# Decode attention beside a gated MLP: the last head's third and fourth V tiles in one load, with dummy matmuls in the wait

## The chip, the core and the metric

The kernel runs on one NeuronCore of a Trainium2 chip. Its engines are the tensor engine (PE; its weight loads are listed as PEld), the vector engine (DVE), the scalar engine (ACT), GpSimd (POOL) and the sync engine (SP), which here issues the large transfers. Sixteen DMA engines bring data from device memory into the on-chip buffer. The metric is the device time of one execution in microseconds (us), taken as the median of several executions. The profile of one execution counts from its first to its last instruction, which is a little less than the device time.

## The reference, cut to what matters

One decode step: a single token `x` of width 1024, attention with 32 query heads over 4 key/value heads of 65,536 positions, and a small gated MLP, mixed by a sigmoid gate.

```python
q = (x @ wq)                                   # 32 heads of 128
k = jnp.repeat(k_cache, 8, axis=1)             # k_cache, v_cache: 4 heads x 65536 x 128, bf16
v = jnp.repeat(v_cache, 8, axis=1)
scores = einsum('bhqd,bhkd->bhqk', q, k) * 128 ** -0.5
p = softmax(scores)
o = einsum('bhqk,bhkd->bhqd', p, v)
a = o.reshape(1, 1, 4096) @ wo                 # wo: 4096 x 1024
# b: the gated MLP of the same token (w_in 1024 x 3584, w_out 1792 x 1024)
out = g * a + (1 - g) * b                      # g = sigmoid(sum(x * gate_w))
```

The two caches are 67 MB each, and the three large weights and `wo` add some 28 MB, all read once.

## The kernel before

The caches are read in tiles of 4 MB (128 partitions x 32 KB), four to a head for K and four for V. All of them, and the weights, go through one buffer `kv` of five such slots. A load names the slot at which it begins and is issued by SP once the earlier users of the slots are done.

```python
kv = big.tile([P, NKV * CT * P], BF16, name="kv")      # NKV = 5 slots, P = CT = 128

def load_kv(src, g, j, at, n=1):                       # n tiles in one transfer, from slot `at`
    ...
    v = load(rows[:, i * CT * DH:(i + n) * CT * DH], (n * CT * DH,), at)
    return [v[:, i * CT * DH:(i + 1) * CT * DH] for i in range(n)]

def v_tile(g, j, vt):                                  # L464: 32 matmuls, 16 weight loads
    for u in range(CC // 2):
        hs = slice(u % 2 * P // 2, (u % 2 + 1) * P // 2)   # two halves of the PE's columns
        for e in range(2):
            nc.tensor.matmul(o_ps[g][hs, e, :], lhsT=ptt[g, j][:, 2 * u:2 * u + 2, :]...,
                             rhs=vx[:, 2 * u + e], ...)    # 128x64 weights, 512 columns

def keep_busy(n):                                      # L503: n matmuls whose result nobody reads
    ps = pss.tile([P, 2 * HN], FP32, name="busy_ps", tag="s")
    ...
    for i in range(n):
        nc.tensor.matmul(ps[:, :HN], lhsT=w[:, :P], rhs=w[:, :HN], start=True, stop=True, ...)
```

`keep_busy` computes nothing: it only keeps PE working, so that its clock isn't lowered. `head_out` ends a head: a masked product of the accumulated output (L474) and a sum (L478) on DVE, two small matmuls (L482 and L484) on PE, and five short DVE operations that end in `oa`, the head's part of the vector that meets `wo`. The tail of the program is:

```python
for j, n, at in ((0, 2, 2), (2, 1, 1), (3, 1, 0)):     # last head's V: tiles 0+1, 2, 3
    for i, vt in enumerate(load_kv(A_v_cache, G - 1, j, at, n)):
        v_tile(G - 1, j + i, vt)
keep_busy(6)
head_out(G - 1)
keep_busy(16)

c0 = 0
for n in WO_SPLIT:                                     # (24, 4, 2, 1, 1) of 32 rows of wo per partition
    t = load(wo_view[:, c0:c0 + n, :], (n, D), 3 + c0 * D / (CT * P))     # from slot 3 on
    project(t, n, oa, c0, last=(c0 + n == OC))         # L514: 4 matmuls of 256 columns per row
    keep_busy(WO_BUSY[n])                              # {24: 0, 4: 2, 2: 1, 1: 0}
    c0 += n
nc.scalar.copy(out=out_sb[:], in_=out_ps[:])           # L566
# two small stores of out_sb
```

[...]SP issues all loads on one queue. The four tiles of the last head's V are called V0 to V3 below.

Of the kernel before, what the change touches and what calls it, by code (L numbers as in the profile page):

```python
# [29 lines left out]
def kernel(  # L30
# [18 lines left out]
    _, G, S, DH = A_k_cache.shape  # L49
# [30 lines left out]
    def same_weights(ins):  # L80
        held.add(ins.ins.name)
# [95 lines left out]
    def load(src, shape, at):  # L177
        n = 1
        for s in shape:
            n *= s  # L180
        v = kv[:, int(at * CT * P):int(at * CT * P) + n]
        if len(shape) == 2:
            v = v.rearrange("p (a b) -> p a b", b=shape[1])
        ins = nc.sync.dma_start(out=v, in_=src)  # L184
        if not first_load:
            first_load.append(ins.ins.name)
        return v

    def load_kv(src, g, j, at, n=1):
        h, i = divmod(j, 2)  # L190
        rows = src[0, g, 2 * h * CT * P:2 * (h + 1) * CT * P, :].rearrange(
            "(p c) d -> p (c d)", c=2 * CT)
        v = load(rows[:, i * CT * DH:(i + n) * CT * DH], (n * CT * DH,), at)
        return [v[:, i * CT * DH:(i + 1) * CT * DH] for i in range(n)]
# [166 lines left out]
    for k in range(NHB):  # L361
# [3 lines left out]
                                                                   j=B, e=2),  # L365
# [91 lines left out]
    def v_tile(g, j, vt):  # L457
        if j == 0:
            o_ps[g] = pso.tile([P, 2, VC * DH], FP32, name="o_ps")
        vx = vt.rearrange("p (v c d) -> p c v d", v=VC, d=DH)  # L460
        for u in range(CC // 2):
            hs = slice(u % 2 * P // 2, (u % 2 + 1) * P // 2)
            for e in range(2):
                ins = nc.tensor.matmul(  # L464
                    o_ps[g][hs, e, :],
                    lhsT=ptt[g, j][:, 2 * u:2 * u + 2, :].rearrange("p c x -> p (c x)"),
                    rhs=vx[:, 2 * u + e], start=(j == 0 and u < 2),
                    stop=(j == NT - 1 and u >= CC // 2 - 2), skip_group_check=True)
                if e > 0:
                    same_weights(ins)  # L470

    def head_out(g):
        gs = slice(g * B, (g + 1) * B)
        nc.vector.tensor_tensor(  # L474
            out=om8, in0=o_ps[g][:].rearrange("p e (v d) -> p (e v) d", d=DH),
            in1=own_8[:].unsqueeze(2).to_broadcast([P, 2 * VC, DH]), op=ALU.mult)
        o_sb = wk.tile([P, DH], FP32, name="o_sb")
        nc.vector.tensor_reduce(out=o_sb[:], in_=om8.rearrange("p x d -> p d x"), axis=AX.X,  # L478
                                op=ALU.add)
        om_ps = psm.tile([P, DH + NT], FP32, name="om_ps", tag="m")  # L480
        hs = hsel[:].rearrange("p h q -> p (h q)")
        nc.tensor.matmul(om_ps[gs, DH:], lhsT=hs, rhs=lss[g][:], start=True, stop=True,  # L482
                         skip_group_check=True)
        nc.tensor.matmul(om_ps[gs, :DH], lhsT=hs, rhs=o_sb[:], start=True, stop=True,  # L484
                         skip_group_check=True)
        rl = wk.tile([P, 2], FP32, name="rl")
        nc.vector.reduce_sum(out=rl[gs, 0:1], in_=om_ps[gs, DH:], axis=AX.X)
        nc.vector.reciprocal(out=rl[gs, 1:2], in_=rl[gs, 0:1])
        om = wk.tile([P, QD, OC], FP32, name="om")
        nc.vector.tensor_tensor(  # L490
            out=om[gs], in0=om_ps[gs, :DH].rearrange("p (q c) -> p q c", c=OC),
            in1=own_q[gs, :].unsqueeze(2).to_broadcast([B, QD, OC]), op=ALU.mult)
        osum = wk.tile([P, OC], FP32, name="osum")
        nc.vector.tensor_reduce(out=osum[gs, :], in_=om[gs].rearrange("p q c -> p c q"),
                                axis=AX.X, op=ALU.add)
        nc.vector.tensor_scalar(out=oa[gs, :], in0=osum[gs, :], scalar1=rl[gs, 1:2],
                                scalar2=gate[gs, :], op0=ALU.mult, op1=ALU.mult)

    def keep_busy(n):
        ps = pss.tile([P, 2 * HN], FP32, name="busy_ps", tag="s")  # L500
        w = wt[G % 2][:].rearrange("p v b t u h -> p (v b t u h)")
        for i in range(n):
            ins = nc.tensor.matmul(ps[:, :HN], lhsT=w[:, :P], rhs=w[:, :HN], start=True,  # L503
                                   stop=True, skip_group_check=True)
            if i > 0:
                same_weights(ins)
# [22 lines left out]
    for g in range(1, G):  # L529
# [16 lines left out]
            if h == 0 and g + 1 < G:  # L546
                build_w(g + 1)
        head_out(g - 1)
    for j, n, at in ((0, 2, 2), (2, 1, 1), (3, 1, 0)):
        for i, vt in enumerate(load_kv(A_v_cache, G - 1, j, at, n)):  # L550
            v_tile(G - 1, j + i, vt)
    keep_busy(6)
    head_out(G - 1)
    keep_busy(16)


    wo_view = A_wo.rearrange("(p c) n -> p c n", c=OC)
# [52 lines left out]
```

## Time and profile before

The time before is 381.88 us, the median of 3 executions (381.71 to 381.96); the profiled span is 380.5 us.

| what | busy us | share of the span |
|---|---|---|
| PE matmuls | 226.4 | 60% |
| PE weight loads | 55.6 | 15% |
| DVE | 211.2 | 56% |
| ACT | 39.6 | 10% |
| POOL | 4.4 | 1% |
| DMA queue of SP | 16 engines | 98.8% |

The DMA engines moved 162.17 MB at a mean of 426 GB/s. Busy time on an engine says little where it works beside another; the reader should first look at which resource has no gaps, and then at the chain of waits that ended last. Granted clock means the share of PE's full clock that the chip allowed it at that moment; in this profile it stands at 1.00 or at 0.50.

### The profile page before, as it was taken

To read this page: it belongs to the slowest core of one execution; us is meant where nothing else is said; L and a number is where in the kernel's file an instruction comes from. 1 tells how busy PE (TensorE), PEld (TensorE's weight loads), DVE (VectorE), ACT (ScalarE), POOL (GpSimd) and SP (SyncE) were. 2 spreads that over 40 slices of the span, in tenths; PEclk is the share of its full clock that TensorE was granted. 3 is DMA by queue.
4 is the path that set the end of the run, shared out by engine and by line. 5 is a ranking of instruction groups with operands and counts; after the bars stand their busy time and mean duration, and the time that the engine had idled before them with its cause. 6 is when DMAs were issued, how large, how long until landed. Compare 5 with 4: busy or idle time off the path is not lost.

```text
span 380.5 us, 2602 instructions
## 1 busy us (share of the span) xinstructions
PE 226.4 (60%) x1397; PEld 55.6 (15%) x800; DVE 211.2 (56%) x207; ACT 39.6 (10%) x55; POOL 4.4 (1%) x10
## 2 busy tenths in 40 slices
PE   0060605967655784794499139762993197739386
PEld 0010101211211210121022001110220011202113
DVE  4134217989374947867893058678940397650040
ACT  1001000111104310114011001140110010500000
POOL 4000000000000000000000000000000000000000
PEclk9995765999958796999599758995898599959789
DMA  9999999999999999999999999999999999999995
GB/s 386 476 420 413 401 442 441 441 472 410 407 422 441 441 443 434 434 434 441 441 429 441 434 441 420 422 413 442 434 434 429 427 434 442 436 410 434 431 432 224
DMA packets 3655, 162.17 MB, mean 426 GB/s; under 512 B 440, under 2 KB 444, under 8 KB 828
## 3 DMA queue, kind: packets, MB, share of 16 engines
q1 hardware_dynamic: 3604, 162.01, 98.8%
q8 instruction: 8, 0.13, 0.1%
q14 instruction: 3, 0.02, 0.0%
q10 hardware_dynamic: 40, 0.01, 0.0%
HBM read 162.01 MB, written 0.00 MB: 426 GB/s over the span
## 4 chain that ended last, share of the span: by engine, by line
DMA 71%; PE 17%; DVE 9%; issue 2%; SPq 0%; ACTq 0%; ACT 0%; DVEq 0%
DMA kv<-in_A_k_cache_dram 52%; PE s_ps L419 13%; DVE kv L412 8%; DMA kv<-in_A_wo_dram 7%; DMA kv<-in_A_v_cache_dram 7%; DMA wb<-in_B_b_sp_dram 5%; PE o_ps L464 2%; PE z_ps L296 1%; SPq L184 0%; DVE mx L402 0%; ACTq L198 0%; PE small_ps L271 0%; ACT out_sb L566 0%; PE out_ps L514 0%; ACTq L199 0%
## 5 line engine op out<-in xcount | busy, mean ns | idle before, releaser
L419 PE MATMUL s_ps<-kv,wt 128*128 128x512 bf16 x512 | 132.8, 414 | 81.4 <-DVE kv L412 81.3
L412 DVE STREAM_TRANSPOSE kv<-kv 128x2048 int32<-128x2048 int32 x64 | 142.4, 2280 | 69.7 <-DMA kv<-in_A_k_cache_dram 69.7
L464 PE MATMUL o_ps<-kv,pt 128*64 128x512 bf16 x512 | 63.6, 408 | 14.3 <-DMA kv<-in_A_v_cache_dram 14.3
L419 PEld LDWEIGHTS <-wt 128*128 128x128 bf16 x256 | 26.4, 103 | 189.2 <-issue 117.9
L428 ACT CAST sc<-s_ps 128x1024 bf16<-128x1024 f32 x16 | 16.2, 1013 | 250.7 <-PE s_ps L419 250.7
L464 PEld LDWEIGHTS <-pt 128*64 128x64 bf16 x256 | 16.9, 117 | 57.9 <-issue 48.6
L454 DVE STREAM_TRANSPOSE pt<-sc 128x1024 bf16<-128x1024 bf16 x16 | 18.6, 1217 | 6.8 <-ACT sc L451 6.8
L474 DVE TENSOR_TENSOR rowt<-o_ps,own 128x1024 f32<-128x1024 f32 x4 | 4.8, 1195 | 26.5 <-PE o_ps L464 26.5
L451 ACT ACTIVATE sc<-sc,nb 128x1024 bf16<-128x1024 bf16 x16 | 18.2, 1137 | 12.2 <-DVE nb L447 12.2
L484 PE MATMUL om_ps<-o_sb,hsel 128*32 128x128 f32 x8 | 2.3, 388 | 18.3 <-DVE o_sb L478 18.3
L402 DVE TENSOR_TENSOR mx<-mx,sc 128x1024 bf16<-128x1024 bf16 x8 | 5.5, 687 | 13.6 <-ACT sc L428 13.6
L296 PE MATMUL q_ps<-kv,xT 128*32 128x512 bf16 x64 | 5.7, 534 | 7.2 <-DMA kv<-in_A_wq_dram 7.2
L252 PE MATMUL xb_ps<-xg,spread 8*128 8x256 bf16 x1 | 0.4, 364 | 13.5 <-DMA xg<-in_gate_w_dram 13.5
L478 DVE TENSOR_REDUCE o_sb<-rowt 128x128 f32<-128x1024 f32 x4 | 7.5, 1872 | 0.1
L363 DVE TENSOR_TENSOR rowt<-q_ps,own_b 128x512 f32<-128x512 f32 x2 | 1.3, 686 | 10.8 <-PE q_ps L296 10.8
L503 PE MATMUL busy_ps<-wt 128*128 128x512 bf16 x25 | 6.1, 381 | 0.0
L296 PE MATMUL z_ps<-kv,xT 128*32 128x448 bf16 x64 | 6.1, 572 | 0.0
L566 ACT CAST out_sb<-out_ps 128x256 bf16<-128x256 f32 x1 | 0.4, 372 | 46.4 <-PE out_ps L514 46.4
L256 DVE TENSOR_TENSOR xm<-xb_ps,sel_i 128x128 f32<-128x128 f32 x2 | 0.5, 286 | 8.2 <-PE xb_ps L252 8.2
L514 PE MATMUL out_ps<-kv,oa 128*32 128x256 bf16 x128 | 4.2, 273 | 1.4 <-DMA kv<-in_A_wo_dram 1.4
L435 DVE TENSOR_REDUCE m<-mx 128x1 f32<-128x1024 bf16 x4 | 4.8, 1209 | 0.1
L296 PEld LDWEIGHTS <-xT 128*32 128x32 bf16 x64 | 2.6, 137 | 14.7 <-issue 14.6
(90 smaller groups left out, 61.2 us busy)
## 6 DMA issues: line engine op xcount, KB each, us to landing
kv<-in_A_v_cache_dram SPq DMA_DIRECT2D x2, 4096.0 KB, 22.8
kv<-in_B_w_in_dram SPq DMA_DIRECT2D x1, 7168.0 KB, 19.7
kv<-in_A_wo_dram SPq DMA_DIRECT2D x1, 6144.0 KB
kv<-in_B_w_out_dram SPq DMA_DIRECT2D x1, 3584.0 KB
kv<-in_A_wo_dram SPq DMA_DIRECT2D x1, 1024.0 KB, 26.8
kv<-in_A_wo_dram SPq DMA_DIRECT2D x1, 512.0 KB
kv<-in_A_wo_dram SPq DMA_DIRECT2D x2, 256.0 KB
kv<-in_A_k_cache_dram SPq DMA_DIRECT2D x8, 27.6
```

Of the source, the lines that this page charges most:

```text
L296: ins = nc.tensor.matmul(ps[t * B:(t + 1) * B, k * HN:k * HN + n], lhsT=xT[:, i * KH + c:i * KH + c + 1].to_broadcast([P, B]), rhs=w[:, c, ...
L402: nc.vector.tensor_tensor(out=mx[:], in0=mxs[g][:], in1=sc[:], op=ALU.max)
L412: nc.vector.transpose(out=kb[:, v * n:(v + 1) * n], in_=kb[:, v * n:(v + 1) * n])
L419: ins = nc.tensor.matmul(s_ps[:, k * HN:(k + 1) * HN], lhsT=wt[g % 2][:, v, b].rearrange("p a v h -> p (a v h)"), rhs=kx[:, b // 2, b % 2, ...
L428: nc.scalar.copy(out=sct[g, j][:], in_=s_ps[:])
L435: nc.vector.reduce_max(out=m1[:], in_=mxs[g][:], axis=AX.X)
L451: nc.scalar.activation(out=sct[g, j][:], in_=sct[g, j][:], func=ACT.Exp, scale=SCALE, bias=nb[:, 0:1], accum_out=lss[g][:, j:j + 1])
L454: nc.vector.transpose(out=ptt[g, j][:].rearrange("p c x -> p (c x)"), in_=sct[g, j][:])
L464: ins = nc.tensor.matmul(o_ps[g][hs, e, :], lhsT=ptt[g, j][:, 2 * u:2 * u + 2, :].rearrange("p c x -> p (c x)"), rhs=vx[:, 2 * u + e], sta ...
L474: nc.vector.tensor_tensor(out=om8, in0=o_ps[g][:].rearrange("p e (v d) -> p (e v) d", d=DH), in1=own_8[:].unsqueeze(2).to_broadcast([P, 2 ...
L478: nc.vector.tensor_reduce(out=o_sb[:], in_=om8.rearrange("p x d -> p d x"), axis=AX.X, op=ALU.add)
L503: ins = nc.tensor.matmul(ps[:, :HN], lhsT=w[:, :P], rhs=w[:, :HN], start=True, stop=True, skip_group_check=True)
```

## The change

Before, V2 and V3 come in two loads of 4 MB, into slot 1 and slot 0. After, they come in one load of 8 MB into slots 0 and 1, as the other V tiles do. PE then has nothing real to do between V1 and the landing of that load, and the change fills the wait with 40 dummy matmuls. The dummies behind V3 stay at 6, and those behind `head_out` go from 16 to 4. The results don't change.

```diff
-    for j, n, at in ((0, 2, 2), (2, 1, 1), (3, 1, 0)):
-        for i, vt in enumerate(load_kv(A_v_cache, G - 1, j, at, n)):
+    for j, at in ((0, 2), (2, 0)):
+        for i, vt in enumerate(load_kv(A_v_cache, G - 1, j, at, 2)):
             v_tile(G - 1, j + i, vt)
-    keep_busy(6)
+        keep_busy((40, 6)[j // 2])
     head_out(G - 1)
-    keep_busy(16)
+    keep_busy(4)
```

The purpose is one transfer fewer, and a PE whose clock is still high when the last two tiles arrive.

## The prediction

> **What bounds the kernel now.** I read the page's 40 slices first, for a resource without gaps; then the chain of waits that ended last, cut to its last stage; then PE's timeline of that stage, for the slack beside the chain; and last the granted clock in chosen stretches, because the change is about dummy matmuls.
>
> The slices and the shares of the chain:
>
> ```profile
> PEclk9995765999958796999599758995898599959789
> DMA  9999999999999999999999999999999999999995
> ...
> DMA 71%; PE 17%; DVE 9%; issue 2%; SPq 0%; ACTq 0%; ACT 0%; DVEq 0%
> ```
>
> The DMA row is at 9 in every slice but the last, while the granted PE clock goes up and down: the transfers run without a pause and PE has room. The last 30 us of the chain (start us, length us, what):
>
> ```profile
> 347.98 0.67 PE o_ps L464 x6
> ...
> 350.46 27.89 DMA kv<-in_A_wo_dram
> 378.35 0.04 issue
> 378.39 0.32 PE out_ps L514 x4
> 378.71 0.02 issue
> 378.73 0.37 ACT out_sb L566
> ```
>
> The end of V1's matmuls at 348.65 frees the slots for wo, and the last wo piece lands at 378.35. Those 27.89 us are a queue, not a start: V2 and V3 were issued at 331.01 and still hold the DMA engines. So the end is set by bytes. Behind the last landing only 4 matmuls, a copy and the stores remain. PE's timeline (start us, length us, then in brackets the idle time before it and what ended it):
>
> ```profile
> 339.43 9.20 PE L464 MATMUL o_ps<-kv,pt 128*64 128x512 bf16 x64 [2.11 <-DMA kv<-in_A_v_cache_dram]
> 349.14 3.65 PE L464 MATMUL o_ps<-kv,pt 128*64 128x512 bf16 x32 [0.52 <-DMA kv<-in_A_v_cache_dram]
> 358.86 6.26 PE L464 MATMUL o_ps<-kv,pt 128*64 128x512 bf16 x32 [6.08 <-DMA kv<-in_A_v_cache_dram]
> ...
> 368.68 3.63 PE L503 MATMUL busy_ps<-wt 128*128 128x512 bf16 x16
> 373.41 3.24 PE L514 MATMUL out_ps<-kv,oa 128*32 128x256 bf16 x112 [1.10 <-DMA kv<-in_A_wo_dram]
> ```
>
> V2 takes 3.65 us and V3, after 6.08 us of idleness, 6.26 us: the lower clock. Yet V3's slowness costs nothing now, because DVE's timeline has `oa` ready at 370.09 (L496, 369.79 + 0.30), and the projection has to wait until 373.41 for wo: 3.3 us of slack.
>
> **The clock.** Sampling the granted clock in steps of 0.25 us shows it falling at 333.5, rising at 343.7, falling at 357.4 and rising at 364.2. The intervals, 10.2, 13.7 and 6.8 us, are 3, 4 and 2 times 3.41 us, and all 22 transitions of the run lie on that grid. The stretches below lie on it (stretch, its length, PE busy time, instructions, granted clock, DMA share, GB/s):
>
> ```profile
> 118.44:121.85 3.41, 1.15 (x7) 1.00 1.20 519
> 121.85:125.27 3.42, 0.00 (x0) 0.50 0.84 364
> 159.41:162.82 3.41, 1.51 (x7) 1.00 1.07 461
> 162.82:166.23 3.41, 2.81 (x13) 1.00 0.98 423
> 330.06:333.47 3.41, 1.07 (x12) 1.00 0.87 370
> 333.47:336.88 3.41, 0.20 (x1) 0.50 1.02 442
> 360.77:364.19 3.42, 3.42 (x19) 0.50 1.03 446
> 364.19:367.60 3.41, 2.49 (x17) 1.00 1.07 461
> 371.01:374.43 3.42, 2.32 (x47) 1.00 0.82 338
> ```
>
> The first stretch was 34% busy and the next one is at half clock; the one at 330.06, 31% busy, likewise. The one at 159.41 was 44% busy and the clock stayed. A full stretch (360.77) brings it back. So this trace puts the limit for a fall between 34% and about 42%, the lowest share in a stretch that stayed up after the start-up.
>
> **What the Trainium skill says.** "TensorE: Matmul & The Clock Gate", Part 1, has a free-running window of 3.4 us at whose end the clock is halved or restored: the grid agrees. It names a whole idle window as what lowers the clock; here 31 to 34% busy did it too, and the measurement decides. The same page ("Wait — 56ns, not 53.3ns?") gives 216 ns per matmul of 512 columns at full clock: the 16 dummies here took 3.63 us, 0.227 each with the last one's tail. "DMA: Bandwidth & Descriptors", "Why a DMA increments its semaphore by 16 and not by 1", says that only the full count means that all data has landed. So V2's matmuls can't begin at half a load. The same page's Bandwidth section fits about 2 us fixed cost for each DMA, on another issue path; here it isn't seen between queued loads: V1, V2 and V3 landed by 339.43, 349.14 and 358.86, 9.71 and 9.72 us apart for 4.19 MB each, which is 431 GB/s.
>
> **The change part by part.**
>
> 1. *The load.* The same 8.39 MB go to the same slots. SP waits for the same event (the previous head's tile leaving slot 1), so issue stays at 331.0, with V0 and V1 still in flight for 8 us. One issue of about 0.4 us goes away on SP, which isn't waited for. As to transfer rate: V2 and V3 took 358.86 - 339.43 = 19.43 us. Two 8 MB loads, from one K landing at 261.97 to the next at 300.67, took 38.70 us, 19.35 each. So fusing saves at most an estimated **0.1 us**.
>
> 2. *V2's matmuls* move from 349.14 to the common landing, about 358.8. 3.65 us that were done early are now done late.
>
> 3. *40 dummies* run from 348.7. Spacing at full clock is (3.63 - 0.38)/15 = 0.217 us (0.38: one matmul's length from the page), so 39 x 0.217 + 0.38 = 8.8 us, to 357.5. That leaves about 1.3 us idle, too little for the clock to fall (at least 60% of any 3.41 us is busy). They end before the landing and delay nothing.
>
> 4. *V2 and V3 at full clock*: 32 matmuls start over 3.45 us (a pair per 0.43 us, with the two column halves overlapping), so 64 take 6.9 + 0.2 = 7.1 us, to 365.9. Before, V3 ended at 365.1. So the restored clock pays back nearly all that fusing costs: net **+0.8 us** here. `head_out` follows unchanged, and `oa` comes at 370.9 instead of 370.1, still 2.5 us ahead of wo. On the end: nothing.
>
> 5. *4 dummies instead of 16* run from 369.5 to 370.5, not to 372.3. Until wo lands at 373.4, PE is idle for 2.9 us, where before it was 1.1 us. Here I see the only way from this change to the end. In a window that closes at time e, PE's busy share falls below 34% for e from about 372.85 to 374.6 (for instance 0.6/3.41 = 18% at e = 373.4). That is 1.75 of 3.41 us, about half of all phases of the free-running grid; for the other half the share is near 40%, at the edge of what I measured. If the clock falls, the projection begins at half rate. At full clock its work, read from the start times of the timeline without the waits, runs 3.17 us for the 112 matmuls, 0.59 for two dummies, 0.33 for 8 matmuls, 0.32 for one dummy, 0.12 and 0.30 for the last two fours: 4.83 us, so PE could be done at 378.24, while it ends at 378.71 (378.39 + 0.32) because of the last landing. That is 0.47 us of slack. Half clock from the landing to the end of one grid stretch lasts 2.9 to 3.4 us and loses half of that, 1.4 to 1.7 us. The end moves by **1.0 to 1.2 us**, and by up to 2.5 if a first stretch of work isn't full enough to restore the clock.
>
> Sum: -0.1 from the load, and a chance of about 0.6 times 1.1 = +0.65 from the clock, on 381.9: **382.4 us**. The 0.6 is my choice: half of the phases for certain, and a small part of the half that stands near 40%.
>
> **Rivals.**
> - *One transfer fewer saves its fixed cost* (2 us): 380. The 9.71 us steps at full rate, and DMA at 9 in every slice, speak against it.
> - *V2 and V3 now collide with the end of the chain*: if the clock falls in the wait nevertheless, 64 matmuls take up to 3.4 us cold and then the rest, some 8.6 us, `oa` comes at 372.5, still before wo. It would take a fully cold 13.8 us to reach 377.7 and an end near 386. The dummies speak against it.
> - *Everything is hidden*: the clock stays up on the 40% windows and with luck of phase, 381.8 us.
> - *Half-clock projection*: 382.8 to 384, as in step 5.
>
> **Range and chances.** The floor is the 0.1 us of the load with some scatter (the runs before span 0.25 us), 381.6; the top is a half-clock projection in the median run, 383.1, with 0.3 us for a slower recovery of the clock, 383.4. Two per cent is 7.6 us, and no term comes near it: same 0.985, faster 0.005, slower 0.01.
>
> **What would show it.** Right: the fused load lands at 358.8 +- 0.2; the 40 dummies end near 357.5; the 64 matmuls take about 7.1 us; L496 ends near 370.9; the last wo piece lands within 0.2 us of 378.3; any added time lies after 373, with clock 0.5 in a stretch there and the x112 group longer than 3.24 us. Wrong: a gap in the DMA row after 348; wo issued more than 5 us later; a landing that moves by over a microsecond; or `oa` later than wo, which would make `head_out` the bound.

## The result, and the profile after

| | median | executions | range |
|---|---|---|---|
| before | 381.87 us | 6 | 381.68 to 381.96 |
| after | 383.32 us | 6 | 382.87 to 384.11 |

The ratio is 1.0042, with a 95% interval from 1.0029 to 1.0055: 1.6 us longer, between 1.1 and 2.1. Within 2% the two count as the same; the difference is nevertheless clear, for no execution of after is as short as any of before. Nor do they agree with each other as those of before do: they spread over 1.24 us against 0.28.

The slices of PE's clock and of the DMA engines, and the shares of the chain that ended last, from the page of after:

```profile
PEclk9995655989969796999599759985898598959996
DMA  9999999999999999999999999999999999999983
...
DMA 62%; PE 19%; DVE 14%; issue 3%; ACT 1%; ACTq 0%; DVEq 0%
```

The DMA row now thins out in its last two slices (8 and 3), where before only the last one was below 9. There is time at the end in which no bytes are awaited. The last stage of the chain of waits (start us, length us, what):

```profile
349.30 23.93 DMA kv<-in_A_wo_dram
373.24 0.04 issue
373.28 6.10 PE out_ps L514 x112
379.38 0.32 PE busy_ps L503
379.70 0.15 issue
379.85 0.40 PE out_ps L514 x8
380.25 0.32 PE busy_ps L503
380.57 0.36 PE out_ps L514 x8
```

The chain leaves the DMA at 373.24, the landing of the first wo piece, instead of at 378.35, the landing of the last one. From there PE's own work is the chain to the end. The first wo piece is not late: PE began the projection at 373.41 before. PE's timeline of after, and below it the line of DVE's that ends in `oa` (start us, length us; in brackets the idle time before and what ended it; x39 stands for the 40 dummies, as a few matmul records are missing from a trace):

```profile
349.20 8.81 PE L503 MATMUL busy_ps<-wt 128*128 128x512 bf16 x39
358.74 7.10 PE L464 MATMUL o_ps<-kv,pt 128*64 128x512 bf16 x64 [0.73 <-DMA kv<-in_A_v_cache_dram]
...
369.40 1.04 PE L503 MATMUL busy_ps<-wt 128*128 128x512 bf16 x4
373.28 6.10 PE L514 MATMUL out_ps<-kv,oa 128*32 128x256 bf16 x112 [2.85 <-DMA kv<-in_A_wo_dram]
...
370.50 0.30 DVE L496 TENSOR_SCALAR oa<-osum,rl,gw 32x32 bf16<-32x32 f32 x1
```

V2 and V3 run at full clock as intended, 7.10 us for 64 matmuls. But 112 matmuls of the projection, which took 3.24 us, take 6.10. The clock shows why. Stretches on the grid of 3.41 us, which in this execution lies elsewhere (stretch, length, PE busy time, instructions, granted clock, DMA share, GB/s):

```profile
365.54:368.96 3.42, 1.80 (x11) 1.00 0.92 393
368.96:372.37 3.41, 1.38 (x6) 1.00 0.77 324
372.37:375.78 3.41, 2.50 (x48) 0.50 0.97 390
375.78:379.19 3.41, 3.41 (x72) 0.50 0.27 102
```

The stretch that ends at 372.37 was 1.38/3.41 = 40% busy, and the clock halves there, a microsecond before wo lands. The next stretch, 73% busy since the projection fills only its later part, doesn't restore it; the one after, completely busy, does, at 379.19. So the projection spends 5.9 us at half clock. PE ends at 380.90 instead of 378.68 (380.50 + 0.40 against 378.39 + 0.29): 2.2 us, which is the difference between the profiled spans, 382.7 and 380.5.

### The profile page after: what moved, and what is told of

The parts are those of the page before. It is cut to its first block, busy times and chain, and to the rows that moved or that the text cites. A ratio compares the mean times of both kernels' runs of the same rounds, so it can differ in the third digit from the quotient of the medians.

```text
span 382.7 us, 2626 instructions
## 1 busy us (share of the span) xinstructions
PE 234.5 (61%) x1422; PEld 57.2 (15%) x801; DVE 211.2 (55%) x207; ACT 39.6 (10%) x55; POOL 4.4 (1%) x10
## 4 chain that ended last, share of the span: by engine, by line
DMA 62%; PE 19%; DVE 14%; issue 3%; ACT 1%; ACTq 0%; DVEq 0%
DMA kv<-in_A_k_cache_dram 45%; PE s_ps L419 12%; DVE kv L412 11%; DMA kv<-in_A_v_cache_dram 7%; DMA kv<-in_A_wo_dram 6%; DMA wb<-in_B_b_sp_dram 5%; PE o_ps L464 4%; PE out_ps L514 2%; DVE pt L454 1%; PE z_ps L296 1%; DVE mx L402 1%; DVE o_sb L478 0%; ACT sc L451 0%; DVE rowt L474 0%; ACT sc L428 0%
## 5 line engine op out<-in xcount | busy, mean ns | idle before, releaser
L419 PE MATMUL s_ps<-kv,wt 128*128 128x512 bf16 x512 | 134.3, 419 | 78.6 <-DVE kv L412 78.4
L464 PE MATMUL o_ps<-kv,pt 128*64 128x512 bf16 x512 | 61.9, 401 | 8.6 <-DMA kv<-in_A_v_cache_dram 8.6
L503 PE MATMUL busy_ps<-wt 128*128 128x512 bf16 x50 | 12.0, 380 | 0.1
L514 PE MATMUL out_ps<-kv,oa 128*32 128x256 bf16 x128 | 6.9, 399 | 3.0 <-DMA kv<-in_A_wo_dram 2.8
L514 PEld LDWEIGHTS <-oa 128*32 128x32 bf16 x128 | 5.1, 139 | 5.3 <-issue 3.0
L296 PE MATMUL z_ps<-kv,xT 128*32 128x448 bf16 x64 | 5.1, 495 | 0.0
```

Of the source, the lines that this page charges most:

```text
L296: ins = nc.tensor.matmul(ps[t * B:(t + 1) * B, k * HN:k * HN + n], lhsT=xT[:, i * KH + c:i * KH + c + 1].to_broadcast([P, B]), rhs=w[:, c, ...
L419: ins = nc.tensor.matmul(s_ps[:, k * HN:(k + 1) * HN], lhsT=wt[g % 2][:, v, b].rearrange("p a v h -> p (a v h)"), rhs=kx[:, b // 2, b % 2, ...
L464: ins = nc.tensor.matmul(o_ps[g][hs, e, :], lhsT=ptt[g, j][:, 2 * u:2 * u + 2, :].rearrange("p c x -> p (c x)"), rhs=vx[:, 2 * u + e], sta ...
L514: nc.tensor.matmul(out_ps[t * B:(t + 1) * B, :], lhsT=vec[:, c0 + c:c0 + c + 1].to_broadcast([P, B]), rhs=w[:, c, t * NO:(t + 1) * NO], st ...
```

## The experiments

Theory A is that of the trace: with 4 dummies PE pauses too long before wo lands, and the projection runs at half clock. Theory B lays the time at the door of the fused load: V2 and V3 multiplied late, or the transfer itself. All comparisons are with the kernel before, on the same chip; its median was 381.82 us in the first four experiments (41 executions) and 381.86 in the next four (30), and the median of its profiled spans 380.3 and 380.4.

**The 16 dummies put back, the load left fused.**

```diff
     head_out(G - 1)
-    keep_busy(4)
+    keep_busy(16)
```

> The changed kernel with 16 dummies behind head_out again instead of 4. Theory A (the clock falls in the 2.85 us pause of PE before wo lands, and the projection then runs at half clock): the pause is gone, the projection starts at full clock, so within 0.3 us of the kernel before, 381.7 to 382.2 us. Theory B (the single 8 MB load, and V2 and V3 being multiplied late, is what costs): nothing changes, 383.0 to 383.6 us.

Measured: 381.83 us, ratio 1.0005 (0.9997 to 1.0013). The whole loss is gone though the load is still one. PE's timeline of this run:

```profile
369.44 3.63 PE L503 MATMUL busy_ps<-wt 128*128 128x512 bf16 x16
373.34 3.24 PE L514 MATMUL out_ps<-kv,oa 128*32 128x256 bf16 x112 [0.27 <-DMA kv<-in_A_wo_dram]
```

The pause is 0.27 us instead of 2.85, and the 112 matmuls are back at 3.24 us. Twelve of the 13 spans are at 380.2 to 380.4; the other, at 381.1, was not profiled. Theory B falls. The run also measures fusing alone: the last wo piece landed at 378.31 against 378.35, and no gain in time can be told from none.

**The loads of before, with only the 16 made 4.**

```diff
     keep_busy(6)
     head_out(G - 1)
-    keep_busy(16)
+    keep_busy(4)
```

> The kernel before, with its two V loads, and only the last number changed: 4 dummies behind head_out instead of 16. Theory A: PE pauses from 369.7 to 373.4, the clock falls whatever its phase, and the time rises by 1.0 to 2.4 us, about 1.6 in the mean: 382.9 to 384.3, median near 383.4 us. Theory B: the loads are those of before, so 381.9 us.

Measured: 383.09 us (382.67 to 383.99), ratio 1.0034 (1.0022 to 1.0047). The last number of the diff alone gives nearly the whole loss, without the fused load; the shortest time lies a little below the 382.9 expected. PE's timeline:

```profile
367.88 1.04 PE L503 MATMUL busy_ps<-wt 128*128 128x512 bf16 x4
373.23 4.77 PE L514 MATMUL out_ps<-kv,oa 128*32 128x256 bf16 x112 [4.31 <-DMA kv<-in_A_wo_dram]
```

Its stretches, with the columns as above:

```profile
366.17:369.58 3.41, 1.38 (x6) 1.00 1.07 461
369.58:372.99 3.41, 0.00 (x0) 0.50 0.72 305
372.99:376.40 3.41, 3.17 (x61) 0.50 0.95 375
```

In this execution the clock fell at 369.6 after a stretch 40% busy and came back at 376.4, so only a part of the projection was slow: 4.77 us, and a span of 381.3.

**The 40 dummies left out.**

```diff
-        keep_busy((40, 6)[j // 2])
+        if j == 2:
+            keep_busy(6)
     head_out(G - 1)
     keep_busy(4)
```

> The changed kernel without the 40 dummies in the wait for V2 and V3. Theory A: V2 and V3 then run partly at half clock and end 2 to 3 us later, but wo lands at 373.3 anyway; the later end shortens the pause in front of the projection, so the clock falls in about half of the executions only: 381.8 to 383.5, median about 382.7 us, faster than the changed kernel. Theory B (late V2 and V3 cost): slower than the changed kernel, by the 2 to 3 us, 385 to 386 us. A third view, that the 40 dummies are what keeps the end fast: also slower.

Measured: 382.37 us (381.57 to 384.11), ratio 1.0021 (1.0007 to 1.0035). With less work done to keep the clock up, the kernel is faster than the changed one in the median, as theory A alone expects, though the intervals of the two ratios overlap; five of the 13 spans are at 380.1 to 380.3. The longest executions went past what I expected: four spans are at 382.2 to 382.7. None of them was profiled, and what they lost is not shown. PE's timeline of the profiled one, with a span of 380.9, shows a second wait:

```profile
359.29 9.94 PE L464 MATMUL o_ps<-kv,pt 128*64 128x512 bf16 x64 [9.97 <-DMA kv<-in_A_v_cache_dram]
...
374.26 3.24 PE L514 MATMUL out_ps<-kv,oa 128*32 128x256 bf16 x112 [0.43 <-DVE oa L496]
```

V2 and V3, at half clock until 365.1, take 9.94 us, and the projection waits for `oa`, at 374.2, no longer for wo, whose first piece landed at 373.8 (issued at 349.4, 24.4 us to its landing). So without the 40 dummies `head_out` can become what the projection waits for once the load is fused, by 0.4 us here. That it cost time at the end isn't shown: in this execution V2 and V3 had already landed at 359.25, half a microsecond later than in the changed kernel's profile, and that alone could make the span 380.9.

**10 dummies behind head_out.**

```diff
-    keep_busy(4)
+    keep_busy(10)
```

> The changed kernel with 10 dummies behind head_out. They end near 371.7, so the pause is 1.6 us. Theory A with the clock falling when a stretch of 3.41 us is less than about 42% busy: no stretch is, so 381.7 to 382.1 us. If even a pause of this length lowers the clock in some phases: 382.3 to 383 us. Theory B: 383.3 us.

Measured: 381.88 us, ratio 1.0004 (0.9997 to 1.0010). PE's timeline of this run:

```profile
373.13 3.24 PE L514 MATMUL out_ps<-kv,oa 128*32 128x256 bf16 x112 [1.55 <-DMA kv<-in_A_wo_dram]
```

The pause is 1.55 us and the 112 matmuls take 3.24 us: this pause costs nothing. All 21 spans lie at 380.1 to 380.6, although single times reach 383.45 us (with a span of 380.3). A part of the scatter of the times is thus outside the profiled span, and where executions are counted below, it is by their spans.

**8 dummies behind head_out.**

```diff
-    keep_busy(4)
+    keep_busy(8)
```

> The changed kernel with 8 dummies behind head_out, between the 4 of the change and the 10 that left no loss. Theory A with a limit of 42% busy in a stretch of 3.41 us: the clock falls in about a third of the phases, so most executions at 381.8 and some at 382.6 to 383.3; median 381.9, mean about 382.2 us. If the number of dummies counted smoothly (4 cost 1.5, 10 cost 0): about 382.3 in every execution.

Measured: 382.82 us, ratio 1.0022 (1.0013 to 1.0032). One of its 17 executions, also the profiled one, ran with a mean clock of 0.757 against 0.834 to 0.852 in the others and is left out of the reading. Of the other 16, seven have a span of 380.2 to 380.5 and nine one of 381.4 to 381.6, with nothing between: an execution either loses 1.1 us or nothing. That is theory A's form, not the smooth one. But the share, nine of 16, is above the third I expected. A single execution for the profile followed:

> The kernel with 8 dummies once more, for a profile whose clock is either full or half. Theory A: either no stretch behind 365 us is under the limit (381.8 us, the 112 matmuls in 3.24 us), or one is, with a busy share of 0.35 to 0.45, and the time is about 1.1 us longer (the 112 matmuls in about 4.7 us).

It took 381.72 us and is one of those that lose nothing, with a pause of 1.98 us:

```profile
373.20 3.24 PE L514 MATMUL out_ps<-kv,oa 128*32 128x256 bf16 x112 [1.98 <-DMA kv<-in_A_wo_dram]
```

**The same 22 dummies, placed ahead of head_out's matmuls.**

```diff
-        keep_busy((40, 6)[j // 2])
+        keep_busy((40, 18)[j // 2])
     head_out(G - 1)
     keep_busy(4)
```

> As many dummies behind V3 as in the run that was fast (22), but 18 of them ahead of head_out's matmuls and only 4 behind. They close the gap in which DVE works (367.2 to 369.1) and leave the pause before wo (371 to 373.3). Theory A: a stretch is below the limit only if it ends near 373 to 374.3, a third of the phases, and the clock then comes back 3.41 us later: most executions at 381.8, a third at 382.5 to 383.1; median about 381.9, mean 382.2. If only the pause in front of wo mattered and not the share of a whole stretch: 383.0 or more in the median, as the changed kernel.

Measured: 382.07 us (381.67 to 383.29), ratio 1.0010 (1.0001 to 1.0019). Eight of 14 spans are at 380.3 to 380.7, six at 381.3 to 381.9. So the number of dummies doesn't decide by itself: 22 of them, with 16 behind `head_out`, lost time in one execution of 13. Nor is a pause of over 2 us in front of wo by itself the loss, as the profiled execution shows, with the stretch in which wo lands (last line, columns as above):

```profile
373.23 3.24 PE L514 MATMUL out_ps<-kv,oa 128*32 128x256 bf16 x112 [2.08 <-DMA kv<-in_A_wo_dram]
...
371.61:375.02 3.41, 1.79 (x68) 1.00 0.91 371
```

The stretch was 1.79/3.41 = 52% busy in spite of the pause, and the clock stayed. Six losses in 14 executions agree with the third that was expected.

**No dummies behind head_out.**

```diff
     head_out(G - 1)
-    keep_busy(4)
```

> The changed kernel with no dummies behind head_out. Theory A: the clock falls at every phase already with 4, so taking them out costs almost nothing more: 382.7 to 384.4, median about 383.4 us. If each dummy saved a fixed part: 383.8 us and above.

Measured: 383.68 us (382.56 to 384.70, four executions), ratio 1.0056 (1.0041 to 1.0071). The interval overlaps that of the changed kernel, and the spans, 381.1 to 382.8, lie where those of the changed kernel do (381.1 to 382.7). So no gain from the 4 dummies that the change left can be seen; four executions are too few to rule out a small one, for the 383.8 us of the other view lies inside the interval.

**The changed kernel once more.**

> The changed kernel once more, for a second phase of its grid. Theory A gives the time of an execution from the moment at which the clock falls behind 365 us: a fall between 370.4 and 372.4 finds a first stretch of the projection that is not full, so the clock returns 6.83 us later and the span is longer than 380.4 by 1.4 to 2.4 us; a fall at 372.9 or later, or at about 369.2, returns 3.41 or 6.83 us later at about 376 to 377 and costs 0.8 to 1.2 us. The median stays at 383.0 to 383.6.

Measured: 383.11 us (382.83 to 383.43), ratio 1.0032 (1.0019 to 1.0045), and a profile with another phase. The same stretches as above:

```profile
369.74:373.15 3.41, 1.38 (x6) 1.00 0.80 335
373.15:376.56 3.41, 3.12 (x60) 0.50 0.91 360
```

And PE's timeline:

```profile
358.90 8.79 PE L464 MATMUL o_ps<-kv,pt 128*64 128x512 bf16 x64 [2.10 <-DMA kv<-in_A_v_cache_dram]
...
373.44 4.75 PE L514 MATMUL out_ps<-kv,oa 128*32 128x256 bf16 x112 [1.16 <-DMA kv<-in_A_wo_dram]
```

Again 40% busy before the fall; but the fall comes at 373.15, just ahead of the projection, so the next stretch is 3.12/3.41 = 91% busy and restores the clock at once. The span is 381.5, 1.1 us above before as foretold for such a fall, against 2.2 for the fall at 372.37. The same kernel costs one or two microseconds by where the grid lies; the spread of its times is of that size. And the pause in front of wo was only 1.16 us here, shorter than the 1.55, 1.98 and 2.08 us that cost nothing above. The stretch also holds the end of PE's wait for `head_out`'s DVE work, before 370.90. So it isn't the pause before wo that decides, but the busy share of a whole stretch of the grid.

## Why the prediction was right or wrong

**Right**, by its steps. The load (step 1): fused data landed at about 358.7, and the runs with 16 and 10 dummies neither gain nor lose by it. V2 and V3 (step 4): 7.10 us as worked out; L496 ended at 370.80 (370.50 + 0.30) against the 370.9 foretold. The way to the end (step 5) is the one named: a fall of the clock in the pause before wo. The rivals of a fixed cost for a transfer, and of `oa` as the bound, didn't come about in the changed kernel. (The fit of about 2 us stands in "DMA: Bandwidth & Descriptors" of the Trainium skill in the section "Anatomy of one DMA — SWDGE (gpsimd) path", not in that on bandwidth; with one transfer fewer and 16 dummies, the ratio to before was 1.0005, so no run here shows such a saving.)

**Wrong** was the size of one term: "a chance of about 0.6 times 1.1 = +0.65 from the clock". With the 0.1 us of the load it gave +0.5 us; measured were 1.45 in the medians. Both factors were too small, and with them step 5, which reckons what the pause of 2.9 us costs.

- *The chance.* I took half of the phases as certain, because their stretch is under 34% busy, and only a small part of the half near 40%. The limit I read from one profile lay "between 34% and about 42%", and I put 40% on the safe side of it. It isn't: the falls at 372.37 and 373.15 above both followed a stretch that was 40% busy. All ten executions of the changed kernel lie above 382.8 us, while the 71 of before in these experiments end at 382.36. The chance was close to 1.
- *The length of the slow spell.* I let half clock last until the end of one grid stretch and kept the longer case for an exception. When the fall comes about a microsecond ahead of wo, as at 372.37, the first stretch is not full enough, and half clock lasts two stretches. Of the two profiles of the changed kernel, one shows 2.2 us for it and the other 1.1. The ten spans are 0.6 to 2.2 us above the 380.5 of before, 1.4 in the mean: close to 1 times 1.4, where I had 0.6 times 1.1.

A smaller slip is in step 3. The 40 dummies begin when V1's matmuls end, and that moves by over a microsecond (347.99 in the second profile of the changed kernel, 349.20 in the first). In the second profile the wait behind them was 2.10 us, not 1.3, the clock did fall in it (at 359.5), and V2 and V3 took 8.79 us. `oa` was then ready at 372.65, still ahead of wo at 373.40.

What is left open is how often 8 dummies lose: nine of 16, where my reckoning with one limit gave a third. An estimate from the profile with 8 dummies: its pause of 1.98 us leaves 1.43 us of work in every stretch that contains all of it, 42% busy and so at the limit itself, and that holds for 1.4 of 3.41 us of placements. The shift of V3's end with the clock in the earlier wait may add to it; no run was made for either. No version found here beats the kernel before: the end is then set by the last bytes of wo.

## What to carry to other kernels

In these runs dummy matmuls were worth something only where real work soon needed the clock. Reckon PE's busy share for every placement of the clock's grid, up to the landing of the data that the next burst of work waits for, and fill until the worst placement is safe. When a change moves work later and trims a filler at the same time, check first whether the filler stood in the way: in the first profile of the changed kernel `oa` was 2.4 us ahead of wo, and the 16 dummies of the first experiment ended before wo landed. They are not safe in every execution, though: with V2 and V3 slow, as in the second profile, 16 dummies from 371.24 would run for 3.63 us to 374.9, past wo at 373.4. That is an estimate, and no profile shows it; 10 dummies (2.33 us) would be through by 373.6, about when wo lands. And where single executions of a kernel fall into two groups, look for something that runs on its own, as the clock's grid does here, before averaging.

## What the runs showed of the hardware

The rule of PE's clock is sharper than I had expected from one profile. I sampled PE's busy time in steps of 0.2 us, from 31 us on, in nine profiles (both kernels and seven of the experiments), and laid it on each profile's own grid of 3.413 us. At full clock, 95 stretches were followed by half clock: the busiest was 41.5% busy (118.12 to 121.54 with 16 dummies and the fused load, 1.42 us of 3.42). 504 were followed by full clock: the least busy of them 40% (236.45 to 239.87 with the loads of before and 4 dummies, 1.37 us of 3.42), and all others 42% or more. At half clock, 206 stretches left it there, with at most 74%, and 103 restored it, with at least 78%. So in these traces the limit for keeping the clock lies at 40 to 42%, where the two groups overlap by a point (a missing matmul record can shift a share), and that for getting it back lies between 74% and 78%. The place of the grid differs from one execution to the next, and with it the cost of the same pause.
